# A searched order for attention and a gated MLP on one core: one early unit's q and k in another buffer, and all order keys drawn anew

## The chip, the cores and the metric

The kernel runs on one core of one Trainium2 chip. The metric is device time in microseconds (us), the median of three runs; the profile comes from one more execution, profiled on its own. The core has five engines: PE (TensorE, matmuls; its weight loads are shown apart as PEld), DVE (VectorE), ACT (ScalarE), POOL (GpSimd) and SP (SyncE, which here issues every DMA).

## The reference, cut to what matters

```python
# q, k, v: (8 batches, 8 heads, 576, 64), float32
scores = q @ k.T / 8                       # heads 0-3: band mask of width 32; heads 4-7: stride mask of 32
attn   = softmax(scores)                   # per row, with the maximum taken off
x      = attn @ v                          # (8, 576, 512) after joining the heads
h      = relu(x @ w_in)                    # w_in 512 x 1024
u, v_  = h[..., :512], h[..., 512:]
v_n    = (v_ - mean) / sqrt(var + 1e-6)    # over the 512 columns
v_s    = w_spatial @ v_n + b_spatial       # w_spatial 576 x 576
out    = (u * v_s) @ w_out                 # w_out 512 x 512
```

## The kernel before, in words

**Units.** Attention is cut into 32 units: unit t = 4 b + hp is head pair hp of batch b. hp 0 and 1 are local (band mask), hp 2 and 3 strided. A local unit's scores are the 72 small matmuls of L522 from its q and k, a strided one's the 64 of L666 from q and `kbd` (k spread over two halves of one tile, half t % 2). Softmax runs on ACT (ten L579 exponentials for a local unit, one L703 for a strided one) and on DVE (L474, L478, L483 normalise, L603 or L720 transposes into the single buffer `pc`). ACT and POOL then copy the transposed blocks to `ptl` or `pts` (L423 on ACT, L425 on POOL), PE multiplies with v into `po` (L632 local, L737 strided), and the result is split into two parts in `x` (an ACT cast L445, the remainder by DVE at L433).

**Batches.** A batch's four `x` are the left side of the v projection (L1034 on PE, 48 matmuls with the v half of `w_in`) and of the u projection (L1102, 96 matmuls with the u half). Then come normalisation, the spatial product (L1206 for batch 0, L1319 after it) and the output product (L1402). Products run on parts: an operand is rounded (L423 or L425) and its remainder kept (L433). The weights arrive in 8-byte words and are converted by L836 (ACT), L844 (POOL) and L852 (DVE), before the same two steps make their parts.

**The order.** Everything is put in a list of operations with their dependences. `Program.order` walks it with costs of its own; of the operations that are ready on an engine, the one with the lowest key goes first, and where an operation may run on several engines it takes the one that ends first. Keys and fetch times come from the table `KEYS` ("a" for units 0 to 7, "la" and "lb" when their loads are issued, "lv", "lu", "wv", "wu" for the weights, and offsets for later stages). The engines run this fixed order; each waits for its operands in turn. `fillers` puts matmuls of zeros (L1630) on PE ahead of an operation for which its plan has a gap.

**Buffers.** q, k and v of local units have one buffer each (rings `r_q`, `r_k`, `r_v`). The early units are declared in the order of their keys "a": 0, 2, 1, 3, 7, 4, 6, 5. Every second one of them among units 0 to 5 (2, 3, 4, 5) takes its q, k and v into slots of `vals`, the tile that appears as `w_out` in the rows, since the output weights come there later. The third early unit is unit 1; its q and k take the second turn of `r_q` and `r_k`, after unit 0. `v4` holds a batch's normalised v; batch 0's is written by L969 after the v projection.

Of the kernel before, what the change touches and what calls it, by code (L numbers as in the profile page):

```python
# [21 lines left out]
HF = DFF // 2  # L22
# [16 lines left out]
CST = 4 * STRIDE + RA + P  # L39
NT = 4  # L40
KEYS = {
    "a": (-48545.87, -36450.5, -36547.42, -23595.43, -3178.89, 14869.6, -2232.61, -3181.02,),
    "v": (10039.16, 14285.99, -10044.91, -16436.95,),
    "u": (11778.77, 13701.39, 14705.78, 15523.81,),
    "s": (-26158.74, 14643.81, 10992.75, 15205.58,),
    "t": (19117.6,),
    "o": (-36501.18, -36627.51,),
    "cst": (-27997.89,),
    "wv": (-36499.87, -14239.13, -2799.46, 1118.56,),
    "wu": (-16432.62, -14796.9, 11768.24, 15524.94,),  # L50
    "lead": (8.83,),
    "fill": (-7882.3, -28137.8, -18899.66, -36412.32, 14186.24, 14826.12,),
    "dp": (854.17, 114.16, 15736.62, 10572.35,),
    "dpt": (3807.98,),
    "lv": (-16503.38, -23194.14, -4424.27, 10590.77,),
    "lu": (18295.16, -11375.3, -4178.09, 15192.78,),
    "lo": (15846.06, -23588.61, 20391.52, 1117.83,),
    "ls": (29744.2, -10984.47, -15240.56, 11983.74, 21527.45,),
    "pre": (7.7, 138.52,),
    "hp": (0.05, 2.03, -16.53, -0.46,),  # L60
    "ol": (-4.44, -4.25, -2.31, -74.96, -289.07, -184.32, 8.51, -6.01,),
    "os": (7.25, 0.33, -27.58, 12.96, 14.34, 74.42, 8.53, 11.2,),
    "vo": (0.15,),
    "uo": (-12.97,),
    "so": (260.06, 79.44, 4.82,),
    "oo": (172.19, 63.89,),
    "to": (-58.13, -3.08, 424.65,),
    "near": (15258.77,),
    "ps": (10.91, -25.52,),
    "tp": (-81.08, 172.34,),  # L70
    "la": (-26458.74, -27118.44, -38717.9, -4867.1, 10591.01, 12736.6, 19276.04, -6157.7,),
    "lb": (-8992.74, -13792.93, -2075.65, -14235.35, 16095.89, 15151.06, -36506.16, -28599.87,),
}
WARM_END, WARM_GAP, WARM_COST, WARM_COLS, WARM_SHARE = 110000.0, 700.0, 427.0, 256, 0.8
PE_MASKED, APART = (0, 1, 2, 3), ()
# [286 lines left out]
def attention_moe(ctx, tc, qT, kT, ks, vl, vs, cst, w_in, w_out, wsp, wtail, out):  # L362
# [4 lines left out]
    ps = ctx.enter_context(tc.tile_pool(name="ps", bufs=1, space=PSUM))  # L367
# [3 lines left out]
    def f32(t):  # L371
        return t.bitcast(F32)
# [27 lines left out]
    r_v4 = Ring(sb, "v4", [P, NT, HF], F32, 1)  # L400
# [28 lines left out]
    def rest(key, n, dst, src, hi, reads, writes, engs=(DVE, POOL), extra=0):  # L429
        cost = {DVE: 70 + 1.04 * n + extra, POOL: 120 + 2.3 * n}  # L430

        def fn(eng):
            eng.tensor_tensor(dst(), src(), f32(hi()), op=ALU.subtract)  # L433

        add(
            key, [(e, cost[e]) for e in engs], fn, reads, writes,
            port=(DVE, POOL) if POOL in engs else (), kind=1,
        )
# [12 lines left out]
    def load(key, dst, src, writes, nbytes, reads=()):  # L451
        add(key, [(DMA, nbytes / DMA_RATE)], lambda eng: eng.dma_start(dst(), src), reads, writes)
# [2 lines left out]
    vals = r_wo.new()  # L455
    early_units = []
    ahead_units = NHP + 2

    def evac_x(due, whole, x_t, o_ps, w, c0, src, dst, extra=0):
        if whole:  # L460
            evac(due - 1, w, lambda: f32(dst(0)), src, [(o_ps,)], [(x_t, 0, c0)], extra=extra)
            return
        evac(due - 1, w, lambda: dst(0), src, [(o_ps,)], [(x_t, 0, c0)], extra=extra)
        rest(
            due - 0.5, w, lambda: dst(1), src, lambda: dst(0),
            [(o_ps,), (x_t, 0, c0)], [(x_t, 1, c0)], (DVE,), extra,
        )
# [291 lines left out]
    def attention(t, due):  # L759
        b, hp = divmod(t, NHP)  # L760
        local = hp < 2
        n = len(early_units)
        early_units.append(t)
        spare = n % 2 and t < ahead_units

        def home(ring, name, width):
            if not spare:
                buf = ring.new()
                return buf, [(buf,)]
            at = VALS + {"q": 0, "k": SP, "v": SP + STRIDE + S}[name]  # L770
            return Slot(vals, lambda w: f32(w).rearrange("p a b c d -> p (a b c d)")[:, at : at + width]), [
                (vals, name)
            ]

        q, qtok = home(r_q, "q", SP)
        if t == 2:
            place = r_t[0].new()
            vtok = [(place,)]
            v = Slot(place, lambda w: f32(w).rearrange("p a b c -> p (a b c)")[:, : NU * D].rearrange(
                "p (u d) -> p u d", d=D  # L780
            ))
        else:
            v, vtok = home(r_v, "v", NU * D)
            if spare:
                v = Slot(v, lambda w: w.rearrange("p (u d) -> p u d", d=D))
        fetch_k, fetch_v = (KEYS[n][t] if t < len(KEYS[n]) else due - d for n, d in (("la", 33), ("lb", 20)))
        load(fetch_k - 1, q, qT[b, hp], qtok, P * SP * 4)
        k = None
        if local:
            k, kin = home(r_k, "k", STRIDE + S)  # L790
            load(fetch_k, k, kT[b, hp], kin, P * (STRIDE + S) * 4)
            load(fetch_v, lambda: v()[:, : 2 * LB, :], vl[b, hp], vtok, P * 768 * 4)
        else:
            for j in range(2):
                load(
                    fetch_k, lambda j=j: kbd[j::2, t % 2, j, STRIDE:],
                    ks[b, hp - 2, j], [("k", t % 2, j)], 64 * S * 4, [("k0", t % 2)],
                )
            load(fetch_v, v, vs[b, hp - 2], vtok, P * 1024 * 4)
            kin = [("k", t % 2, j) for j in range(2)]  # L800
        (local_attention if local else strided_attention)(t, due, q, k, v, vtok, kin, qtok)

    def x_tok(t):
        return [(xs[t], i, c0) for i in range(1 if t in WHOLE else 2) for c0 in ((0, 3) if t % NHP < 2 else (0, 1))]
# [211 lines left out]
    def turn(b):  # L1016

        return sorted(range(NHP), key=lambda hp: due(NHP * b + hp))

    def v_tile(key, step, x_at, m, toks, kts, b=None):  # L1020
        v_ps = r_pm.new(held)
        for n, kt in enumerate(kts):
            val, vtok = in_value(1, kt)
            whole = b is not None and NHP * b + kt in WHOLE
            given = [vtok] if whole else [("w_in", 1, kt, 0), ("w_in", 1, kt, 1)]

            def f(eng, n=n, kt=kt, val=val, whole=whole):
                if whole:
                    eng.matmul(
                        v_ps()[:m, :], f32(x_at(kt)[:, 0, :]), val(), start=n == 0, stop=n == NT - 1,  # L1030
                    )
                    return
                for i, (a, w) in enumerate(PROD):
                    eng.matmul(  # L1034
                        v_ps()[:m, :],
                        x_at(kt)[:, a, :],
                        w_in_sb[:, w, kt, HF:],
                        start=(n == 0 and i == 0),
                        stop=(n == NT - 1 and i == 2),
                    )  # L1040

            add(
                key + step * n, [(PE, whole_cost(512) if whole else 3 * pe_cost(m, 512))], f,
                toks(kt) + given, [(v_ps,)],
                spare=None if n else (v_ps, v_ps),
            )
        return v_ps

    vns, v4s, tls, us = {}, {}, {}, {}

    def flat(u):
        return u() if u.ring is r_u else f32(u()).rearrange("p a b -> p (a b)")
# [1 line left out]
    def by_tile(buf):  # L1054
        return lambda w: buf()[:, w].rearrange("p a b -> p (a b)")[:, :HF]
# [2 lines left out]
        return lambda: v4()[:, 2 * j : 2 * j + 2, i * HF // 2 : (i + 1) * HF // 2]  # L1058

    def project_v(b, key):  # L1060
        v4 = v4s[b] = r_v4.new()
        if b not in FAST_S:
            vns[b] = [(r_g if i < NT - 1 else r_t[2]).new() for i in range(NT)]
        for i in range(NT):
            k0 = key + 2.6 * i
            v_ps = v_tile(
                k0, 0.65,
                lambda kt, i=i: xs[NHP * b + kt]()[:, :, i * P : i * P + P],
                P, lambda kt: x_tok(NHP * b + kt), turn(b), b,
            )  # L1070
            v = lambda i=i: v4()[:, i]
            chain(k0 - KEYS["vo"][0], v_ps, P, v, [(v4, i, 0), (v4, i, 1)], b > 0 and i in ACT_NORM)
            if b not in FAST_S:
                at, buf = by_tile(vns[b][i]), vns[b][i]
                rnd(k0, HF, lambda at=at: at(0), v, [(v4, i, 0), (v4, i, 1)], [(buf, 0)])
                rest(
                    k0, HF, lambda at=at: at(1), v, lambda at=at: at(0),
                    [(v4, i, 0), (v4, i, 1), (buf, 0)], [(buf, 1)],
                )
# [433 lines left out]
    lead = min(nb, 2)  # L1513
# [199 lines left out]
```

## Time and profile before

| | |
|---|---|
| median of three runs | 512.02 us (510.07 to 512.26) |
| the profiled execution, its own time | 512.99 us |
| its span, first to last instruction | 511.2 us |
| PE busy | 489.7 us, 96% of the span |
| DVE, ACT, POOL busy | 381.3, 302.9, 183.4 us |
| mean granted TensorE clock | 0.983 |

The profiled execution takes 1.8 us more than its span, and 0.97 us more than the median. [...]

### The profile page before, as it was taken

What the parts mean: (1) busy time and instruction counts of PE and PEld (TensorE: products, weight loads), DVE (VectorE), ACT (ScalarE), POOL (GpSimd) and SP (SyncE); (2) the same over time, 40 slices, a digit from 0 to 9 for tenths busy, and PEclk for the clock granted to TensorE, in tenths of its full rate; (3) what the DMA queues carried; (4) which work ended last, traced back from release to release, by engine and by line L of the source; (5) the groups of instructions that cost most, each with busy time, mean ns of one, the idle gap of its engine ahead of it and who ended that gap; (6) DMA issues with size and microseconds to landing.
All of it is one profiled execution on the core that took longest, in us unless ns stands there. A gap on an engine that the chain in (4) does not pass through costs nothing.

```text
span 511.2 us, 15881 instructions
## 1 busy us (share of the span) xinstructions
PE 489.7 (96%) x6316; PEld 447.3 (88%) x6316; DVE 381.3 (75%) x1119; ACT 302.9 (59%) x935; POOL 183.4 (36%) x298
## 2 busy tenths in 40 slices
PE   7489999999999999999999999999999999999996
PEld 4367989898897999989998999989998999889996
DVE  3868887699998866999288964999469852966175
ACT  4857685777567777547555676637654643334333
POOL 4753541323655741545125240445216121222010
PEclk9579999999999999999999999999999999999999
DMA  8957132642513542506040252504120040002002
GB/s 312 401 204 257 44 107 84 223 131 90 184 50 96 174 115 81 167 2 196 20 129 0 76 198 81 161 7 158 59 80 1 9 171 1 1 0 94 1 1 94
DMA packets 26970, 54.48 MB, mean 107 GB/s; under 512 B 3216, under 2 KB 11536, under 8 KB 26896
## 3 DMA queue, kind: packets, MB, share of 16 engines
q1 hardware_dynamic: 26896, 53.47, 32.2%
q8 instruction: 50, 0.82, 0.7%
q14 instruction: 24, 0.20, 0.1%
HBM read 44.02 MB, written 9.44 MB: 105 GB/s over the span
## 4 chain that ended last, share of the span: by engine, by line
PE 77%; DVE 9%; DMA 5%; POOL 2%; ACT 2%; issue 2%; SPq 1%; DVEq 0%; POOLq 0%; ACTq 0%
PE m L1102 18%; PE m L1034 16%; PE m L1402 15%; PE m L1319 13%; PE po L632 3%; PE po L737 3%; PE m L1206 2%; DMA q<-qT 2%; PE s L522 2%; PE m L1173 2%; PE s L666 2%; PE m L1174 2%; DMA g<-w_in 1%; DVE g L433 1%; DVE g L867 1%
## 5 line engine op out<-in xcount | busy, mean ns | idle before, releaser
L1102 PE MATMUL m<-x,w_in_sb 128*128 128x288 f32 x768 | 104.6, 296 | 0.6 <-issue 0.6
L1102 PEld LDWEIGHTS m<-x,w_in_sb 128*128 128x128 f32 x768 | 102.7, 189 | 1.4 <-issue 0.8
L1034 PE MATMUL m<-w_in_sb,x 128*128 128x512 f32 (+1 forms) x408 | 101.2, 404 | 0.0
L1402 PE MATMUL m<-g,w_out 128*128 128x288 f32 x672 | 95.1, 298 | 2.1 <-DVE o L1425 0.9
L1402 PEld LDWEIGHTS m<-g,w_out 128*128 128x128 f32 x672 | 90.5, 188 | 5.2 <-DVE g L433 1.5
L1034 PEld LDWEIGHTS m<-w_in_sb,x 128*128 128x128 f32 (+1 forms) x408 | 75.9, 189 | 19.2 <-DVE x L433 0.3
L423 ACT CAST g<-u 128x288 fp32r<-128x288 f32 x85 | 36.2, 433 | 34.7 <-DVE u L867 16.6
L1319 PE MATMUL m<-wsp_sb,g 128*128 128x288 f32 x336 | 51.2, 298 | 0.1
L579 ACT ACTIVATE pl<-pl,ml 128x64 f32<-128x64 f32 (+1 forms) x140 | 47.1, 340 | 2.8 <-DVE ml L559 2.6
L425 POOL TENSOR_SCALAR ptl<-pc 32x64 f32<-32x64 f32 (+3 forms) x95 | 37.2, 392 | 31.4 <-DVE pc L603 14.7
L1319 PEld LDWEIGHTS m<-wsp_sb,g 128*128 128x128 f32 x336 | 46.6, 188 | 1.2 <-ACT u L445 0.3
L433 DVE TENSOR_TENSOR x<-po,x 128x288 fp32r<-128x288 f32 x64 | 26.9, 445 | 24.5 <-ACT x L445 24.3
L987 POOL TENSOR_TENSOR bn<-bn,sel 128x1 f32<-128x1 f32 (+1 forms) x37 | 23.0, 625 | 61.7 <-DVE bn L982 57.7
L433 DVE TENSOR_TENSOR g<-u,g 128x288 fp32r<-128x288 f32 x77 | 38.4, 519 | 3.5 <-ACT g L423 1.8
L1319 PE MATMUL m<-wsp_t,g 128*128 128x288 f32 x252 | 39.6, 296 | 1.1 <-ACT o L445 1.1
L423 ACT COPY ptl<-pc 32x320 f32<-32x320 f32 (+3 forms) x97 | 34.4, 356 | 10.2 <-DVE pc L603 8.5
L1116 ACT ACTIVATE u<-m 128x288 f32<-128x288 f32 x56 | 22.3, 408 | 30.4 <-PE m L1102 29.5
L433 DVE TENSOR_TENSOR g<-v,g 128x512 fp32r<-128x512 f32 x40 | 27.6, 691 | 13.5 <-ACT g L423 9.6
L969 ACT ACTIVATE v<-m 128x512 f32<-128x512 f32 x32 | 18.8, 597 | 31.0 <-PE m L1034 30.5
L1319 PEld LDWEIGHTS m<-wsp_t,g 128*128 128x128 f32 x252 | 35.4, 188 | 1.5 <-ACT o L445 1.3
L445 ACT CAST x<-po 128x288 fp32r<-128x288 f32 x60 | 22.2, 398 | 22.9 <-PE po L632 11.9
L445 ACT COPY o<-m 128x288 f32<-128x288 f32 x74 | 29.1, 398 | 8.7 <-PE m L1319 7.0
(168 smaller groups left out, 856.3 us busy)
## 6 DMA issues: line engine op xcount, KB each, us to landing
q<-qT SPq DMA_DIRECT2D x28, 295.0 KB, 3.3
v_raw<-vs SPq DMA_DIRECT2D x14, 512.0 KB, 4.1
v_raw<-vl SPq DMA_DIRECT2D x14, 384.0 KB, 3.7
kbd<-ks SPq DMA_DIRECT2D x32, 144.0 KB, 3.8
outT<-o SPq DMA_DIRECT2D x32, 144.0 KB, 3.0
k<-kT SPq DMA_DIRECT2D x14, 304.0 KB, 4.6
outT<-u SPq DMA_DIRECT2D x28, 144.0 KB, 2.5
g<-w_in SPq DMA_DIRECT2D x5, 512.0 KB, 5.9
```

The costliest lines, as they stand in the source:

```text
L423: eng.copy(dst(), src())
L425: eng.tensor_scalar(dst(), src(), 1.0, 0.0, op0=ALU.mult, op1=ALU.add)
L433: eng.tensor_tensor(dst(), src(), f32(hi()), op=ALU.subtract)
L445: eng.copy(dst(), src())
L579: eng.activation(p_sb()[:m, u, :], src, AF.Exp, bias=st()[:m, u : u + 1], scale=SCALE if masked else -1.0, **total,)
L969: lambda eng: eng.activation(v()[:m], v_ps()[:m, :], AF.Relu), [(v_ps,)], toks,
L987: lambda eng: eng.tensor_tensor(bn()[:m, 9:10], bn()[:m, 8:9], sel[:m, 0:1], op=ALU.pow),
L1034: eng.matmul(v_ps()[:m, :], x_at(kt)[:, a, :], w_in_sb[:, w, kt, HF:], start=(n == 0 and i == 0), stop=(n == NT - 1 and i == 2),)
L1102: eng.matmul(u_ps()[:, :HS], w_in_sb[:, w, kt, f * P : (f + 1) * P], xs[NHP * b + kt]()[:, a, r], start=(n == 0 and i == 0), stop=(n == NT ...
L1116: lambda eng, u=u, f=f, u_ps=u_ps: eng.activation(flat(u)[:, f * HS : (f + 1) * HS], u_ps()[:, :HS], AF.Relu),
L1319: eng.matmul(banks[j]()[:, :HS], buf()[:, a, r, P * j : P * j + P], at(w, r), start=first and r == 0 and i == 0, stop=tail is None and r = ...
L1402: eng.matmul(o_ps()[:, :HS], w_out_t[0]()[:, w, r, BLOCKS[name], j * P : (j + 1) * P], at(a), start=(first and r == 0 and i == 0), stop=(r ...
```

## The change

Two things change. First, unit 1's q and k go to a buffer that is idle until the v projection of batch 0 writes it: `v4`. The ring turn of `r_q` and `r_k` that they leave falls to the next unit that asks for one. Second, all numbers of `KEYS` are others. Shapes, formulas and the list of operations stay as they are. Lines below the new code move down (L579 is L580, L1034 is L1039, L1102 is L1109, L1630 is L1637).

```diff
-    "a": (-48545.87, -36450.5, -36547.42, -23595.43, -3178.89, 14869.6, -2232.61, -3181.02,),
+    "a": (-44893.87, -34918.54, -34921.08, -31255.24, -3190.06, 13718.87, -503.41, -3191.92,),
...
-    "la": (-26458.74, -27118.44, -38717.9, -4867.1, 10591.01, 12736.6, 19276.04, -6157.7,),
+    "la": (-44251.4, -34909.86, -37998.29, -4144.15, 13982.3, -34242.77, -34705.02, -39685.72,),
...
+    v4s = {0: r_v4.new()}
...
         def home(ring, name, width):
+            if n == 2 and name != "v":
+                i = "qk".index(name)
+                flat_v = lambda w: w.rearrange("p a b -> p (a b)")[:, 2 * HF * i : 2 * HF * i + width]
+                return Slot(v4s[0], flat_v), [(v4s[0], 2 * i + r, j) for r in range(2) for j in range(2)]
...
-    vns, v4s, tls, us = {}, {}, {}, {}
+    vns, tls, us = {}, {}, {}
...
     def project_v(b, key):
-        v4 = v4s[b] = r_v4.new()
+        if b not in v4s:
+            v4s[b] = r_v4.new()
+        v4 = v4s[b]
```

**The loads on SP.** The first loads of the program, before, from the conversion of the first weight block on; `q_188` and `k_190` are unit 1's, `u`, `g` and `wsp_t` take weights, `x` takes rows of `wsp`, `w_out` is `vals`:

```order
L452 DMA u_102<-w_in 128x1024
L452 DMA kbd<-ks 64x576 x2
L452 DMA g_107<-w_in 128x1024
L452 DMA x_113<-wsp 128x576
L452 DMA w_out_84<-vs 128x1024
L452 DMA u_132<-w_in 128x1024
L452 DMA x_142<-wsp 128x576
L452 DMA v_raw_180<-vl 128x768
L452 DMA kbd<-ks 64x576 x2
L452 DMA q_188<-qT 128x590
L452 DMA k_190<-kT 128x608
```

The first loads of the changed program; unit 1's are those into `v_0_124`, the `v4` tile:

```order
L1548 DMA cst_sb<-cst 128x274
L452 DMA q_89<-qT 128x590
L452 DMA k_95<-kT 128x608
L452 DMA g_98<-w_in 128x1024
L452 DMA w_out_103<-qT 128x590
L452 DMA kbd<-ks 64x576 x2
L452 DMA x_111<-wsp 128x576
L452 DMA v_0_124<-qT 128x590
L452 DMA v_0_124<-kT 128x608
L452 DMA x_138<-wsp 128x576
```

Unit 1's k is the ninth load instead of the fifteenth (a row marked x2 is taken as one), and one weight block stands ahead of it instead of three.

**PE around the first product with v.** Before, the end of unit 1's scores, unit 0's product with v, the scores of unit 3, the first v projection matmuls and unit 2's product with v:

```order
L522 MATMUL m_137<-k_190,q_188 32x64
L632 MATMUL po_328<-ptl,v_raw_180 64x96 x6
L632 MATMUL po_339<-ptl,v_raw_180 64x96 x6
L666 MATMUL m_140<-kbd,w_out_84 32x36 x32
L1034 MATMUL m_400<-w_in_sb,x_352 128x512 x3
L737 MATMUL po_412<-pts,wsp_t_0_231 64x2x18
```

The same place of the changed program:

```order
L523 MATMUL m_135<-v_0_124 32x64
L1637 MATMUL po_334<-zeros 32x256 x10
L633 MATMUL po_334<-ptl,v_raw_198 64x96 x6
L633 MATMUL po_355<-ptl,v_raw_198 64x96 x6
L667 MATMUL m_140<-kbd,w_out_103 32x36 x32
L1039 MATMUL m_419<-w_in_sb,x_367 128x512 x3
L738 MATMUL po_426<-pts,wsp_t_0_180 64x2x18
```

Ten rows of zero matmuls now stand between unit 1's scores and unit 0's product. Those that stood further on (three rows and two, around the scores of units 7 and 4) are two rows now; in all there are 20 such rows instead of 13. The numbers of all other matmuls are equal line by line.

**ACT after unit 0's softmax.** Before, from the copies of unit 0's transposed blocks (`pc_274`) to the first two exponentials of unit 1 (`m_134`, `m_137`):

```order
L423 COPY ptl<-pc_274 32x10x32 x3
L423 COPY ptl<-pc_274 32x8x32
L423 COPY ptl<-pc_274 32x4x32
L423 COPY ptl<-pc_274 32x2x32
L423 CAST w_in_sb<-w_out_84 128x512
L836 ACTIVATE g_228<-g_228 128x512
L445 CAST x_352<-po_328 128x288
L445 CAST x_352<-po_339 128x288
L423 COPY pts<-pc_346 32x16x18 x3
L579 ACTIVATE pl_77,ml_79<-m_134,ml_79 128x64
L579 ACTIVATE pl_77,ml_79<-m_137,ml_79 128x64
```

The same place of the changed program (`m_132` and `m_135` are unit 1's scores):

```order
L423 COPY ptl<-pc_300 32x10x32 x3
L423 COPY ptl<-pc_300 32x8x32
L423 COPY ptl<-pc_300 32x4x32
L423 COPY ptl<-pc_300 32x2x32 x2
L580 ACTIVATE pl_77,ml_79<-m_132,ml_79 128x64
L423 CAST wsp_sb<-x_138 128x2x288
L580 ACTIVATE pl_77,ml_79<-m_135,ml_79 128x64
```

Unit 1's exponentials now follow the copies at once; two casts of `wsp_sb` and, after the fifth of them, the two casts of unit 0's `x` lie between the ten. Between the copies of unit 1's own blocks and the casts of its `x`, ACT has five weight operations now, where there was one. On PE, the scores of unit 5 (36 pairs) now stand ahead of the first L1102, where they stood after the 24th; from there on the order on PE is the same but for places at which attention units cut in. Over the whole program DVE has 30 operations more (15 of L433, 8 of L867, 4 of L483 among them), POOL 29 two-input ones fewer and 9 of L425 more, ACT 11 casts and copies fewer.

## Rows read from the trace of the kernel before

**Rows 1.** Windows: us, busy time (instructions) of PE, PEld, DVE, ACT, POOL; clock, DMA share, GB/s.

```profile
10.00:20.00 10.00, 1.49 (x89) 1.16 (x75) 8.71 (x19) 7.45 (x30) 6.03 (x8) 0.65 1.03 406
20.00:30.00 10.00, 7.76 (x159) 6.58 (x160) 6.75 (x15) 7.07 (x31) 7.52 (x12) 0.67 1.04 395
99.00:146.00 47.00, 45.34 (x569) 41.32 (x568) 44.87 (x124) 33.97 (x96) 20.57 (x24) 1.00 0.39 126
215.55:333.01 117.46, 116.88 (x1566) 109.10 (x1565) 89.71 (x274) 71.07 (x228) 41.80 (x69) 1.00 0.31 95
```

**Rows 2.** What PE waited for over the whole span: us in total, times, longest.

```profile
PE m L522 <- DMA k<-kT: 7.7, 1, 7.7
PE po L737 <- issue: 2.2, 1, 2.2
```

**Rows 3.** PE in order of time: start us, us, line, tiles, count, wait before.

```profile
17.89 1.34 PE L522 MATMUL m<-k,q 64*32 64x64 f32 x72 [7.74 <-DMA k<-kT]
20.00 2.19 PE L632 MATMUL po<-ptl,v_raw 128*64 128x96 f32 x24 [0.77 <-POOL ptl L425]
28.34 7.49 PE L1034 MATMUL m<-w_in_sb,x 128*128 128x512 f32 x21
37.92 1.21 PE L632 MATMUL po<-ptl,v_raw 128*64 128x96 f32 x24
49.69 3.35 PE L1102 MATMUL m<-x,w_in_sb 128*128 128x288 f32 x24
52.97 1.14 PE L737 MATMUL po<-pts,v_raw 64*64 64x36 f32 x64
54.04 0.97 PE L522 MATMUL s<-w_out 64*32 64x64 f32 x72
444.85 11.27 PE L1034 MATMUL m<-w_in_sb,x 128*128 128x512 f32 x48
```

**Rows 4.** ACT, POOL and DVE in order of time, 17 to 35 us.

```profile
17.47 0.65 ACT L423 CAST wsp_sb<-x 128x576 fp32r<-128x576 f32 x1
18.05 2.43 ACT L423 COPY ptl<-pc 32x320 f32<-32x320 f32 x6
21.61 0.37 ACT L445 CAST x<-po 128x288 fp32r<-128x288 f32 x1
23.88 0.32 ACT L579 ACTIVATE pl<-m,ml 128x64 f32<-128x64 f32 x1
24.18 0.30 ACT L579 ACTIVATE pl<-m,ml 128x64 f32<-128x64 f32 x1
30.00 0.21 ACT L579 ACTIVATION_READ_ACCUMULATOR pl<-m,ml 64x1 f32 x1
33.09 3.01 POOL L425 TENSOR_SCALAR ptl<-pc 32x320 f32<-32x320 f32 x6
17.16 0.80 DVE L603 STREAM_TRANSPOSE pc<-pl 128x640 f32<-128x640 f32 x1
```

**Rows 5.** Windows as in rows 1, after PE's two idle stretches.

```profile
13.00:14.00 1.00, 0.00 (x0) 0.00 (x0) 0.09 (x1) 1.00 (x7) 0.84 (x3) 0.50 1.03 394
28.00:30.00 2.00, 2.00 (x15) 1.64 (x12) 1.23 (x3) 1.66 (x10) 0.32 (x1) 0.50 1.05 396
```

**Rows 6.** DMA issues, 0 to 45 us: tiles, count, KB each, median us to landing.

```profile
v_raw<-vl SPq DMA_DIRECT2D x2, 384.0 KB, 6.3
w_out<-kT SPq DMA_DIRECT2D x2, 304.0 KB, 6.9
```

**Rows 7.** The issue of unit 1's v on SP.

```profile
25.36 0.33 SPq L452 DMA_DIRECT2D v_raw<-vl  x1
```

**Rows 8.** DVE and POOL in order of time, at 130 and 56 us.

```profile
130.49 1.52 DVE L483 TENSOR_TENSOR pp<-pp,mx 128x288 f32<-128x288 f32 x1
130.41 1.29 POOL L867 TENSOR_TENSOR v<-v 128x512 f32<-128x512 f32 x1
56.03 0.46 DVE L483 TENSOR_TENSOR pp<-pp,mx 128x288 f32<-128x288 f32 x1
```

More of the change, by code (lines that the diff above doesn't have):

```diff
@@ L41 @@
 KEYS = {
-    "a": (-48545.87, -36450.5, -36547.42, -23595.43, -3178.89, 14869.6, -2232.61, -3181.02,),
[L43 to L70, printed above, removed]
-    "la": (-26458.74, -27118.44, -38717.9, -4867.1, 10591.01, 12736.6, 19276.04, -6157.7,),
-    "lb": (-8992.74, -13792.93, -2075.65, -14235.35, 16095.89, 15151.06, -36506.16, -28599.87,),
+    "a": (-44893.87, -34918.54, -34921.08, -31255.24, -3190.06, 13718.87, -503.41, -3191.92,),
@@ new lines @@
+    "v": (-2810.29, -12128.07, -1687.49, -26558.84,),
+    "u": (15964.95, 29527.72, 31760.64, 13043.35,),
+    "s": (-48288.31, -44892.86, -43645.28, -36128.68,),
+    "t": (42175.42,),
+    "o": (-1614.63, -5723.49,),
+    "cst": (-45514.64,),
+    "wv": (-44071.37, -32108.45, 46701.81, 53190.54,),
+    "wu": (44641.61, 14489.25, -184.6, -43642.99,),
+    "lead": (7.63,),
+    "fill": (14244.08, 13201.8, -35181.89, -35007.95, -2621.23, -4291.2,),
+    "dp": (1227.9, 12.48, 13438.64, 63416.92,),
@@ new lines @@
+    "dpt": (5145.73,),
+    "lv": (-41706.16, 19747.99, -26450.31, 44752.58,),
+    "lu": (44814.44, 13716.43, -34900.79, 45439.75,),
+    "lo": (44767.72, -36135.43, -26015.77, 14700.03,),
+    "ls": (-1873.27, -35726.72, -3193.89, -29206.82, 38692.31,),
+    "pre": (0.98, 201.19,),
+    "hp": (1.46, 17.46, -19.6, -1.05,),
+    "ol": (-4.81, -1.97, -83.56, -15.28, -397.63, -173.59, 15.76, -6.31,),
+    "os": (9.38, 7.77, -42.16, 23.46, 13.5, 112.89, -7.83, -202.64,),
+    "vo": (-10.95,),
+    "uo": (122.84,),
@@ L73 @@
+    "so": (146.17, 90.75, 224.33,),
+    "oo": (32.37, 5.7,),
+    "to": (-84.46, -4.52, 320.0,),
+    "near": (57359.77,),
+    "ps": (2.8, -110.71,),
+    "tp": (-462.02, 508.05,),
+    "la": (-44251.4, -34909.86, -37998.29, -4144.15, 13982.3, -34242.77, -34705.02, -39685.72,),
+    "lb": (-2534.85, 13906.78, -7006.51, 42261.49, -45191.78, -40284.21, 13014.5, -747.88,),
 }
```

## The prediction

> **What bounds the kernel now.** I read the windows first, then PE's waits, then the order in time on each engine. PE is busy 489.7 of 511.2 us. In the steady batches it has nothing left to give: in the 117.46 us of two batches it works 116.88 [rows 1]. Nearly all that can be won lies in the first 50 us: from 10 to 20 us PE works 1.49 us, and its one long wait of the program is 7.74 us for the k of unit 1 [rows 1 to 3]. After that it is slow as well as late: the granted clock is 0.65 to 0.67 between 10 and 30 us [rows 1], and 21 matmuls of the v projection take 7.49 us, 357 ns each, where 48 at full clock take 11.27, 235 ns each [rows 3]. A wait of 2.2 us with no releaser lies in unit 2's product with v [rows 2]. The DMA engines are full from 10 to 30 us, at 395 to 406 GB/s [rows 1], so what comes first in SP's order comes first on the chip. A second tight place is 99 to 146 us, where DVE works 44.87 of 47 us and PE loses 1.66 [rows 1].
>
> **Unit 1's q and k.** What stands ahead of and with unit 1's k in SP's order is, by the sizes of the loads, 5214 KB before (q and k of unit 0, q and v of unit 2, two kbd pairs, three weight blocks, two of wsp, unit 0's v, the constants) and 2718 KB after. The 2496 KB between them are 2.56 MB; at 406 GB/s that is 6.3 us. k landed when PE's wait ended, at 17.89 [rows 3], and so should land at 11.6. Unit 2's scores end at about 10.1 (17.89 less the wait), so PE waits some 1.5 us, not 7.74, and unit 1's scores end near 12.5. This alone moves nothing that PE must finish later: unit 0's product, next in order, waits for its softmax.
>
> **Unit 0's product.** Its transpose starts at 17.16 [rows 4], behind other steps of DVE. One weight step of about 0.7 us has gone from ahead of it and a reduction of unit 1 of half that has come. I take 0.4 us sooner, so PE starts it at 19.6, not 20.00.
>
> **Unit 1's softmax is the real term.** Before, its first exponential runs at 23.88, after the copies, two weight steps, two casts of x and three copies for unit 2; its last accumulator read ends at 30.21 [rows 4]. Now ACT copies seven blocks at 405 ns each (2.43 us for six [rows 4]) from 17.6 on, to 20.4. Then come ten exponentials at 0.30 (23.88 to 24.18 is one step), two wsp casts at 0.65 and two x casts at 0.37: 3.0 + 1.3 + 0.75 [rows 4], which ends at 25.45, 4.8 us sooner. From there to the end of the copies of unit 1's blocks it took 5.9 us before (30.21 to 33.09 + 3.01 [rows 4]); the same now gives 31.3. Unit 1's v has the same bytes ahead of it as before, about 10.5 MB, and was issued at 25.36; with 6.3 us to landing it comes at 31.7 [rows 6, 7]. I take 31.5 for unit 1's product, against 37.92 [rows 3], where PE came 1.8 us after the copies because it was held up by the slow v projection.
>
> **From there to the u projection.** PE's work, at full clock: the products of units 1 and 3 at 1.1 each, scores of units 4 and 5 at 0.9 (unit 5's row has 0.97, with the overlap into what follows [rows 3]), those of units 7 and 6 at 0.8 (64 matmuls for 72), and 24 matmuls at 235 ns, 5.6: 11.2 in all. One wait is new: the casts of unit 1's x stand behind five weight steps on ACT of about 0.6 us. They can't start before 34.3 (31.3 + 3.0), while PE is through with unit 7's scores at 33.4; with the casts and the remainder, PE waits 1.5. So the first L1102 starts at 31.5 + 11.2 + 1.5 = 44.2. Before it is 49.69, and unit 5's scores, 0.9, are still to come at 54.04 [rows 3]. The gain at this landmark is 5.5 + 0.9 = 6.4 us. Its bounds: PE's own work from 19.6, with nothing waited for, is 11.2 + 8.6 (two products 2.2, unit 3's scores 0.8, 24 matmuls 5.6) and 0.9 of zeros, which ends at 40.3, a gain of 10.3; and if the 2.2 us and the low clock (below) come back in full, it is 1.5.
>
> **The clock.** The zeros after unit 1's scores are 20 instructions, 4.3 us at full clock, so they end at 16.8 and PE then idles until 19.6. [...] Unit 0's product took 2.19 at the low clock where unit 1's took 1.21 [rows 3]; over some 5.5 us of low clock that is 2.75 us of work lost. Most of it lies under the wait for unit 1's softmax and for ACT's five steps, which ends at 34.3 whatever PE does; I charge 0.6, between 0 and 2.75. [...]
>
> **Unit 5's scores.** They stand ahead of the whole u projection now, and PE works in order: 96 matmuls wait behind them, and DVE's and ACT's work on u behind those. Their q and k go to slots that unit 4's scores free, 5.6 us of matmuls and 0.7 of unit 6's scores earlier. Issued one after the other, the second lands 6.9 us after [rows 6] at the pace of the full queue, and in about 4 when it isn't full. I charge 0.5, between 0 and 2.
>
> **DVE from 99 to 146 us.** Everything in it hangs on weights whose buffers PE frees, so it moves with PE. It holds about three operations more, 0.45 each, 1.35 us; against that, by the order, five of POOL's steps fewer run beside it. A normalising step took 1.52 us beside a POOL step, 0.46 elsewhere [rows 8]. [...] I charge 0, from -1.66 (PE's loss there gone) to +1.35.
>
> **The rest.** From 150 us on PE does the same matmuls; the 27 or so DVE operations that come in addition, some 13 us, fall on an engine that is busy 89.71 of 117.46 us [rows 1], under PE's work. I charge 0.
>
> **The sum.** -6.4 + 0.6 + 0.5 = -5.3 us: 512.99 becomes 507.7 for an execution like the profiled one, and 512.02, the median, 506.7.
>
> **The rivals.**
> - *The front gives less*, because the 2.2 us come back as they were (the wait stands where small matmuls follow each other while the DMA engines are full, which is still so) and the clock costs its whole 2.75. Then 6.4 - 2.2 - 2.75 + 1 for what is hidden under ACT = 2.45, less 0.5: about 510.
> - *The front gives more*: softmax of unit 1 isn't held by v or by ACT, PE runs through from 19.6. With 8 to 10 us, about 503. Against it speaks that v's bytes come no sooner.
> - *The change doesn't do what it seems to*: the gain of the front is lost again between 60 and 150 us, because DVE has no slack there (rows 1 give 2.13 us in 47). Then 512. Against it: the work there starts when PE frees buffers, and DVE idles much before 50 us.
> - *Slower*: the work taken from POOL makes DVE the bound of the steady batches. It decides if DVE's 89.71 us per two batches, with 3 to 4 more, come to stand in front of PE: each operation on which PE then waits adds its 0.45 us. Half of the 27 would cost 6 us and undo the front; all of them, 12, gives 518.5. PE's idle time there, 0.58 in 117.46, shows no sign of it.
>
> **How the numbers follow.** What a measurement of this kernel can tell from no change is about 0.5%, 2.56 us. The forecast (505 to 508.5) has 0.55; less from the front (508.5 to 511) 0.20, of which half is under 509.46; more from the front 0.10; the gain lost later 0.08; slower 0.07. Faster is then 0.55 + 0.10 + 0.10 = 0.75, same 0.18, slower 0.07. The range leaves the last two cases out and a part of the second: 501.5 to 510.8. The likeliest case alone is 505 to 508.5.
>
> **What would show it.** PE's wait for k gone or under 2 us; unit 1's product at 30 to 33 us; the first L1102 at 42.5 to 46; the clock at 0.50 for a few us after 19; the span from the first L1102 to the end equal to before less 0.9 us, within 1.5. I am wrong if unit 1's product comes after 35, if PE waits over 2 us for unit 5's q or k, or if PE's idle time after 60 us grows by more than 2 us.

## The result, and the profile after

| | median, us | runs |
|---|---|---|
| kernel before, measured beside it | 509.95 (509.24 to 512.26) | 6 |
| changed kernel | 514.75 (514.43 to 516.46) | 6 |

The ratio is 1.0088, with a 95% interval of 1.0061 to 1.0115: slower by 4.8 us, where 506.7 was forecast. The profiled execution took 514.52 us, with a span of 512.7.

The front went much as forecast. PE's order in time, changed kernel, from the end of the first scores to the u projection (start, length, engine, line, operation, tiles, count, and the wait before it):

```profile
10.93 0.80 PE L523 MATMUL m<-v 64*32 64x64 f32 x59 [1.07 <-DMA v<-kT]
15.25 0.46 PE L523 MATMUL m<-v 64*32 64x64 f32 x13 [3.52 <-issue]
15.64 6.25 PE L1637 MATMUL po<-zeros 128*32 128x256 f32 x20
21.83 1.21 PE L633 MATMUL po<-ptl,v_raw 128*64 128x96 f32 x24
...
26.57 5.18 PE L1039 MATMUL m<-w_in_sb,x 128*128 128x512 f32 x21
...
32.66 1.21 PE L633 MATMUL po<-ptl,v_raw 128*64 128x96 f32 x24
...
44.91 0.97 PE L523 MATMUL s<-w_out 64*32 64x64 f32 x72
45.81 2.65 PE L1109 MATMUL m<-x,w_in_sb 128*128 128x288 f32 x18
```

The tile that holds unit 1's q and k goes by the name `v` here. Against [rows 3], the wait for k is 1.07 us, not 7.74; unit 1's product starts at 32.66, not 37.92; the u projection at 45.81, not 49.69, with unit 5's scores done. One line should have puzzled me: 20 zero matmuls took 6.25 us and ended at 21.8, where I had them end at 16.8.

The loss is later. PE's waits over the whole program, changed kernel (what PE waited for, total us, times, longest):

```profile
PE po L738 <- DMA v_raw<-vs: 3.6, 3, 2.0
PE m L523 <- issue: 3.5, 1, 3.5
PE m L1409 <- DVE g L433: 1.6, 3, 0.7
...
PE po L738 <- DVE ml L560: 0.9, 1, 0.9
PE s L523 <- issue: 0.9, 1, 0.9
PE po L633 <- DMA v_raw<-vl: 0.7, 1, 0.7
```

The first line has no counterpart in [rows 2], nor among the other waits of the kernel before: three times PE waits, in a strided unit's product, for the load of its v. Two more waits of this kind stand in other lines. One is the last line, of a local unit, at 169.81 us. The other is the 0.9 us put down to `DVE ml`, at 300.07 us: that product reads no `ml`, and its v landed at 299.94. It starts 0.14 us after that landing, as the other four start 0.13 to 0.14 us after theirs. The five waits add up to 5.2 us. The longest, in PE's order around 237 us, and behind it SP's order there:

```profile
229.60 1.21 PE L633 MATMUL po<-ptl,v_raw 128*64 128x96 f32 x24
230.74 1.85 PE L1409 MATMUL m<-g,w_out 128*128 128x288 f32 x12
232.43 2.93 PE L1109 MATMUL m<-x,w_in_sb 128*128 128x288 f32 x21
237.35 1.70 PE L738 MATMUL po<-pts,v_raw 64*64 64x36 f32 x64 [1.98 <-DMA v_raw<-vs]
238.98 1.15 PE L523 MATMUL s<-k,q 64*32 64x64 f32 x61
241.02 0.45 PE L523 MATMUL s<-k,q 64*32 64x64 f32 x11 [0.90 <-issue]
241.41 5.62 PE L1109 MATMUL m<-x,w_in_sb 128*128 128x288 f32 x30
246.96 1.14 PE L738 MATMUL po<-pts,v_raw 64*64 64x36 f32 x64
```
```profile
229.70 0.34 SPq L452 DMA_DIRECT2D q<-qT  x1
230.14 0.85 SPq L1440 DMA_DIRECT2D outT<-o  x2
231.10 0.42 SPq L452 DMA_DIRECT2D v_raw<-vs  x1
231.61 0.91 SPq L1440 DMA_DIRECT2D outT<-o  x2
232.65 0.84 SPq L1440 DMA_DIRECT2D outT<-u  x2
233.55 1.66 SPq L452 DMA_DIRECT2D kbd<-ks  x2
```

`v_raw` is one buffer. It comes free when the product before it ends, at 230.8 (229.60 + 1.21); the load is issued at 231.10, and PE has only 4.6 us of other matmuls until 235.4. The load lands at 237.21, 6.1 us after its issue, among a q load, six stores of 144 KB and two key loads. In the kernel before, unit 17's product stands ahead of the v projection, and the same load has 15.7 us until unit 18's product (PE, then SP):

```profile
209.87 1.21 PE L632 MATMUL po<-ptl,v_raw 128*64 128x96 f32 x24
215.39 11.27 PE L1034 MATMUL m<-w_in_sb,x 128*128 128x512 f32 x48
228.20 1.14 PE L737 MATMUL po<-pts,v_raw 64*64 64x36 f32 x64
```
```profile
212.45 0.52 SPq L452 DMA_DIRECT2D v_raw<-vs  x1
```

The new keys put unit 17's product behind the projection (208.1 to 219.3 us in the changed kernel), and so next to unit 18's. A short hand-over alone is not yet a wait: at 289.56 the kernel before ends such a product and starts the next at 293.96 without one. Its load, the first transfer issued on SP since 265 us, took 3.9 us.

In the changed kernel the low clock follows the wait: the strided product at 237.35 takes 1.70 us, not the 1.14 of the one at 246.96. The windows say why (us, length, PE busy and instructions, granted clock, of which 1.00 is full speed, DMA share, GB/s):

```profile
236.00:238.00 2.00, 0.65 (x35) 0.92 0.99 361
238.00:240.00 2.00, 2.00 (x101) 0.50 0.13 46
240.00:242.00 2.00, 1.10 (x22) 0.50 0.72 250
242.00:244.00 2.00, 2.00 (x11) 0.50 0.71 189
245.00:247.00 2.00, 2.00 (x20) 1.00 0.02 9
```

The clock falls to 0.50 some 0.3 us after the end of the wait (0.84 from 237 to 238 us) and stays there until 244.5 (0.75 from 244 to 245). To see what such places cost in all, I added up the matmuls that each traced execution had started by a given time, each at its spacing at full clock (a 288-column one 139 ns, a 512-column one 235, the small ones 12 to 50; zeros left out), and took off the same sum for the kernel before. This is the lead in us, here for the profiled executions of this change and of five experiments below:

```
at us   changed   e5 (before   e9 (no   e7 (place  e6 (products  e11 (new front,
        kernel     again)      zeros)    alone)       later)       old rest,
                                                                   2 moves)
  50      4.3        1.2        -0.4      -0.1         5.5           3.7
 150      5.9        2.0         0.0       0.0         7.1           5.1
 230      5.9        1.8        -0.4       0.0         7.5           4.9
 250     -0.2        2.1        -0.3       0.0         6.4           5.1
 310     -1.0        1.4        -0.5      -0.3         4.8           4.8
 370     -2.5        1.5        -1.0      -0.3         4.3           4.9
 500     -2.4        1.5        -1.1      -0.3         3.0           4.4
```

The changed kernel leads by 5.9 us until 230, loses 6.1 of it by 250, 0.8 more by 310 (0.91 us at 300.07 and 0.19 at 305.60, both for loads of v) and 1.5 by 370 (1.46 for a load of v at 360.22; there the clock stays at 1.00). A trace is one execution: the front of the changed kernel, of e6 and of e11 is the same, and yet the three lead by 5.9, 7.1 and 5.1 us at 150.

### The profile page after: what moved, and what is told of

Same layout as the page of the kernel before. It is cut to its first block, busy times and chain, and to the rows that moved or that the text cites. A ratio compares the mean times of both kernels' runs of the same rounds, so it can differ in the third digit from the quotient of the medians.

```text
span 512.7 us, 15896 instructions
## 1 busy us (share of the span) xinstructions
PE 492.5 (96%) x6330; PEld 448.2 (87%) x6330; DVE 386.5 (75%) x1149; ACT 302.7 (59%) x926; POOL 155.9 (30%) x277
## 4 chain that ended last, share of the span: by engine, by line
PE 73%; DVE 12%; DMA 7%; issue 2%; ACT 2%; POOL 1%; SPq 1%; POOLq 0%; DVEq 0%; ACTq 0%
PE m L1039 16%; PE m L1109 16%; PE m L1326 14%; PE m L1409 11%; PE po L738 3%; DMA v_raw<-vs 3%; DVE g L433 3%; PE po L633 2%; PE s L523 2%; PE m L1213 2%; DMA g<-w_out 2%; PE m L1180 2%; PE m L1181 1%; PE po L1637 1%; DVE g L872 1%
## 5 line engine op out<-in xcount | busy, mean ns | idle before, releaser
L1109 PE MATMUL m<-x,w_in_sb 128*128 128x288 f32 x768 | 107.9, 299 | 0.0
L1109 PEld LDWEIGHTS m<-x,w_in_sb 128*128 128x128 f32 x768 | 104.1, 191 | 1.2 <-issue 0.2
L1039 PE MATMUL m<-w_in_sb,x 128*128 128x512 f32 (+1 forms) x408 | 98.6, 397 | 0.4 <-DVE x L433 0.4
L1409 PE MATMUL m<-g,w_out 128*128 128x288 f32 x672 | 94.0, 297 | 2.7 <-DVE g L433 1.6
L1039 PEld LDWEIGHTS m<-w_in_sb,x 128*128 128x128 f32 (+1 forms) x408 | 74.4, 185 | 19.3 <-DVE x L433 0.8
L425 POOL TENSOR_SCALAR ptl<-pc 32x64 f32<-32x64 f32 (+3 forms) x100 | 38.9, 389 | 62.0 <-DVE pc L604 29.8
L580 ACT ACTIVATE pl<-pl,ml 128x64 f32<-128x64 f32 (+1 forms) x140 | 47.1, 339 | 3.2 <-DVE ml L560 2.9
L433 DVE TENSOR_TENSOR g<-v,g 128x512 fp32r<-128x512 f32 x44 | 30.9, 704 | 16.0 <-ACT g L423 13.1
L433 DVE TENSOR_TENSOR g<-u,g 128x288 fp32r<-128x288 f32 x85 | 38.2, 466 | 2.7 <-POOL g L425 1.4
L992 POOL TENSOR_TENSOR bn<-bn,sel 128x1 f32<-128x1 f32 (+1 forms) x37 | 24.1, 655 | 51.6 <-DVE bn L987 39.7
L445 ACT CAST x<-po 128x288 fp32r<-128x288 f32 x58 | 21.8, 400 | 28.0 <-PE po L633 14.0
L433 DVE TENSOR_TENSOR x<-po,x 128x288 fp32r<-128x288 f32 x64 | 27.3, 446 | 12.1 <-ACT x L445 12.0
L423 ACT COPY ptl<-pc 32x320 f32<-32x320 f32 (+3 forms) x92 | 33.1, 360 | 4.1 <-DVE pc L604 2.3
L423 ACT CAST g<-v 128x512 fp32r<-128x512 f32 x34 | 21.1, 621 | 21.1 <-PE m L1326 8.5
```

The lines of the kernel that those rows point to most:

```text
L423: eng.copy(dst(), src())
L425: eng.tensor_scalar(dst(), src(), 1.0, 0.0, op0=ALU.mult, op1=ALU.add)
L445: eng.copy(dst(), src())
L580: eng.activation(p_sb()[:m, u, :], src, AF.Exp, bias=st()[:m, u : u + 1], scale=SCALE if masked else -1.0, **total,)
L992: lambda eng: eng.tensor_tensor(bn()[:m, 9:10], bn()[:m, 8:9], sel[:m, 0:1], op=ALU.pow),
L1039: eng.matmul(v_ps()[:m, :], x_at(kt)[:, a, :], w_in_sb[:, w, kt, HF:], start=(n == 0 and i == 0), stop=(n == NT - 1 and i == 2),)
```

## The experiments

Except for e5, the order is written out as a table, operation by operation, taken from the planner of one kernel or the other, and edited there; the planner no longer chooses:

```diff
-        issued = self.order()
-        fillers = self.fillers(issued)
+        issued, fillers = written(), FILLS
```

With the table in it, line numbers in their rows are 81 higher (L738 is L819, L1109 is L1190). No run leaves work out. With the moved operations of PE, a few of ACT or DVE move too (e6, e8, e11, e13), and two or three output stores on SP (e8, e11, e13). Medians, each with the kernel before on the same chip (509.7 to 510.0 us in each set):

| run | us | runs | ratio to before, 95% |
|---|---|---|---|
| e1 new front, old rest | 509.88 | 12 | 0.9992 (0.9968 to 1.0016) |
| e2 old front, new rest | 522.0 | 4 | 1.0209 (1.0163 to 1.0256) |
| e3 new, stores later | 511.7 | 10 | 1.0035 (1.0005 to 1.0064) |
| e4 new, 16 zeros in the wait | 514.29 | 10 | 1.0074 (1.0047 to 1.0102) |
| e5 before again | 512.05 | 1 | |
| e6 new, products later | 511.25 | 10 | 1.0022 (1.0001 to 1.0042) |
| e7 old, placement alone | 511.75 (511.23 without one at 516.0) | 10 | 1.0024 (0.9997 to 1.0051) |
| e8 as e1, scores later | 507.58 | 12 | 0.9952 (0.9933 to 0.9971) |
| e9 as e8, no zeros | 511.89 | 12 | 1.0036 (1.0014 to 1.0059) |
| e10 new, 8 zeros in the wait | 512.58 | 10 | 1.0047 (1.0021 to 1.0072) |
| e11 as e8, a product later too | 506.1 | 6 | 0.9923 (0.9892 to 0.9953) |
| e12 e7 with 20 zeros | 511.21 | 12 | 1.0022 (0.9994 to 1.0051) |
| e13 e12 with e11's two moves | 507.73 | 12 | 0.9968 (0.9948 to 0.9987) |
| e14 as e11, 14 zeros | 510.04 | 12 | 0.9984 (0.9958 to 1.0011) |

**Front or rest? e1, e2.** The two orders are joined at about 150 us of the planner's time; what one had not yet done by then follows in the other's order.

> The new kernel's order up to about 150 us, then the order of the kernel before for all that is left. Theory A (the front gains 5 us and keeps them; the new order loses them at three places after 230 us, where PE waits for a v load): 504 to 506 us beside 509.95 for the kernel before. Rival B (whatever the front wins is taken back in the steady batches, because another engine or the queue sets their pace): 509 to 511.

> The other way round: the kernel before up to about 150 us, then the new order. Theory A (the loss belongs to the later order and doesn't depend on the lead; it is 5.9 us between 230 and 250 us and about 2.4 more by 370): 516.5 to 518.5 us. Rival B (the steady batches only absorb a lead that the front made): 510 to 512, no worse than before.

e2's profiled execution, 517.69, is where theory A put it: by the sum of the table above, its lead goes from 4.8 us at 230 to -4.4 at 500. Its three others, and so its median, are above A's range, at 521.4 to 524.2. Their mean granted clock is 0.977 to 0.980 against 0.987, which means 7 to 11 us more at 0.50, by an estimate from unit 0's product (2.19 us at 0.50, 1.21 at 1.00) some 3 to 5 us of work; where that happens no trace shows. So the new rest costs time whatever stands before it. But e1 is no faster than the kernel before: A fails there. In its traced execution (511.5 us, 1.6 above the median) the lead stays at 5.2 to 5.5 us from 150 to 270 and is 0.6 by 310. PE's order there, and the DMA queues during the wait (packets, MB, share):

```profile
290.20 0.90 PE L604 MATMUL s<-k,q 64*32 64x64 f32 x69 [0.35 <-DMA q<-qT]
293.13 0.42 PE L604 MATMUL s<-k,q 64*32 64x64 f32 x3 [2.04 <-issue]
```
```profile
q1 hardware_dynamic: 544, 0.85, 97.2%
q8 instruction: 1, 0.02, 2.6%
```

In the middle of unit 24's scores PE waits 2.04 us for nothing that a semaphore shows, while the data queue holds 97.2% of the DMA engines and one 16 KB packet of instructions comes through; the clock is 0.88 from 291 to 293 us, and 0.50 from 293 to 298 (for 6.8 us in all). I call such waits instruction waits, after that packet (the expectations of e9 and e13: waits for instructions); that PE waits for it is not shown. The lead is lost at one place, not worn down.

**The load: e3, e6.**

```diff
 SP order, at both places (units 18 and 26)
-  q, store o x2, v_raw, store o x2, store u x2, kbd x2, v_raw, q, k
+  q, v_raw, kbd x2, store u x2, v_raw, q, k, store o x4
```

> The new kernel, with the output stores that surround two v loads of strided units (issued at 231.10 and 354.49) put behind later loads in SP's order. Theory A1 (the load lands late, after 6.1 us, because it shares the DMA engines with six stores): it lands in 4 to 4.5 us, PE's waits of 1.98 and 1.46 us and the 0.50 clock after the first are gone, 506.5 to 508.5 us. Rival B1 (the order asks for the product too soon after the buffer comes free, the stores don't matter): the waits stay over 1 us and the time is 513.5 to 515.

Neither, quite: at 354 us the wait shrinks from 1.46 to 0.18 us, at 237 only from 1.98 to 1.23. There the load still takes 5.6 us, not 6.1, with the q load just ahead and the key loads just behind: the stores are a small part of its time. What the larger part is was not tested. The clock stays at 1.00 (the product takes 1.14 us and the 30 u matmuls behind the scores 4.24, not 1.70 and 5.62), and 3.0 us come back.

```diff
 PE order, at both places
-  product 18, scores 20, u x7 groups, ...
+  u x7 groups, product 18, scores 20, ...
-  product 19, scores 21, u x8 groups
+  u x8 groups, product 19, scores 21
```

> The new kernel with nothing changed in SP's order, but with the two strided products and the scores behind them put 7 to 9 groups of u matmuls later in PE's order, in the two batches where PE waited 1.98 and 1.46 us. Theory A (PE comes to the product sooner than a load issued 5 us earlier can land; nothing else is wrong): both waits and the 0.50 clock at 237.7 go, 507.5 to 510 us. Rival B (the later work is short of something else, and the loss comes back at another place): 513 to 515.

The two waits are gone and the clock doesn't fall (unit 18's product, at 236.52, takes 1.14 us; the mean clock is 0.993 against 0.987); 3.5 us come back. The median, 511.25, is 1.25 us above A's range, so A is right about the waits and wrong that nothing else costs. Its trace still shows, beyond 200 us, waits of 0.20 (243), 0.23 (245) and 0.58 us (294) for loads, of 0.49 for DVE (267 and 386) and 0.36 for ACT (369), and behind 430 us the three that the kernel before has too. The one at 294 goes by `DVE ml` again; its v landed at 294.34 and the product starts at 294.48.

**The clock after the wait: e4, e10.** Zeros (L1637) go ahead of unit 18's product, as the planner does in the front. "8" in e4's text became 16 instructions, 3.64 us, too long by 1.7; e10 has 8.

> The new kernel with 8 zero matmuls in PE's order ahead of the strided product that waits 1.98 us, so that PE works through most of that wait. Theory A2 (of the 6.1 us lost there 3 to 4 are the clock of 0.50 that follows, the wait itself is the smaller part): the clock stays 1.00 and the time is 510.5 to 512. Rival B2 (the wait and what it delays are the whole loss): 514 to 515.5.

> The new kernel with zeros ahead of the product that waits 1.98 us, half as many as in the run with zeros before: 8 instructions, some 1.8 us, as long as the wait itself. If the clock that fell after the wait is worth 2.6 to 3.5 us: the clock is 1.00 from 237 to 245 us and the time 511 to 512.5 us. If the earlier zeros only moved the loss: 514 to 515.

PE in e10, same place:

```profile
236.48 1.91 PE L1718 MATMUL po<-zeros 128*32 128x256 f32 x8
238.33 1.14 PE L819 MATMUL po<-pts,v_raw 64*64 64x36 f32 x64
239.40 0.76 PE L604 MATMUL s<-k,q 64*32 64x64 f32 x53
240.95 0.41 PE L604 MATMUL s<-k,q 64*32 64x64 f32 x19 [0.79 <-issue]
241.29 4.24 PE L1190 MATMUL m<-x,w_in_sb 128*128 128x288 f32 x30
245.47 1.14 PE L819 MATMUL po<-pts,v_raw 64*64 64x36 f32 x64
```

From the product to the next one it is 7.14 us, where the changed kernel takes 9.61 (246.96 - 237.35), with nearly the same instruction wait: the low clock alone cost 2.4 us (2.47 less 0.11 of instruction wait), more than the wait of 1.98. The median fell by 2.2, a little short of the first theory's range. e4 keeps the clock at 1.00 there as theory A2 says (1.14 us for the product and 4.24 for the 30 u matmuls, as in e10), but its median, 514.29, falls into B2's range: the same gain less the overrun of 1.7 would be 0.5, and that is what it gives, too little to tell from none with these runs.

**What the front is worth: e5, e7.**

> The kernel before, profiled a second time. Theory C (the profiled execution that the prediction was built on was a slow one: its clock fell a second time, at 26.6 us, and that is 3 to 4 us of the front that most executions don't lose): the clock stays 1.00 from about 22 us on, the first L1102 starts at 45 to 47 us and the span is 506 to 508 us. Rival D (that front is the kernel's own): the first L1102 at 49 to 50 us and a span near 511.

> The order of the kernel before, with q and k of the third early unit in the v buffer and their two loads put where the change has them, ahead of the weights in SP's order; nothing else moves. By the prediction's step (the wait for k alone holds up nothing that PE must finish later, since the product of unit 0 waits for its softmax): PE's wait of 7.7 us for k is under 2 us, the product of unit 0 still starts at 19.5 to 20.5 us and the time is 509 to 510.5. Rival E (the wait for k holds the front): the first L1102 is 3 to 6 us earlier than in the kernel before and the time 504 to 507.

e7 is as the prediction's step had it: wait for k 1.51 us, unit 0's product at 20.11, the first L1102 at 49.80, no gain. Its median, 511.75, is above the step's range of 509 to 510.5, and its clock falls twice, as in the first trace (2.19 us for unit 0's product, 7.21 for the 21 matmuls behind unit 2's; the mean is 0.983 in both). e5 lies between, its span of 510.3 us nearer to D: the product with v of unit 2 waits 1.77 us without a releaser, the clock falls again at 27.2 (0.57 from 27 to 31 us), but for 3.4 us, not 6.8, and the first L1102 starts at 48.43. e2 begins with the same old order, and there the clock didn't fall a second time (0.92 from 20 to 30 us, 1.00 from 30 to 40; 5.42 us for the 21 matmuls), after a wait of 1.99 us in the same product:

```profile
26.20 0.89 PE L818 MATMUL po<-pts,wsp_t 64*64 64x36 f32 x43 [1.99 <-issue]
27.02 5.42 PE L1115 MATMUL m<-w_in_sb,x 128*128 128x512 f32 x21
...
34.55 1.21 PE L713 MATMUL po<-ptl,v_raw 128*64 128x96 f32 x24
...
45.87 3.35 PE L1183 MATMUL m<-x,w_in_sb 128*128 128x288 f32 x24
```

So one order gives 45.87, 48.43 and 49.69 for the same landmark. The execution that I predicted from was at the slow end: of 121 executions of the kernel before in the five sets, 6 took as long as its 512.99 us, and 11 had a mean granted clock as low as its 0.983 (511.05 to 514.21 us); the 74 at 0.988 and above have a median of 509.1.

**Out of the stall: e8, e11.**

```diff
 PE order of e1
-  scores 24, o x2 groups, u x6 groups
+  o x2 groups, u x6 groups, scores 24          (e8: 8 groups)
-  product 30, o x2 groups, u x3 groups
+  o x2 groups, u x3 groups, product 30         (e11: 5 groups, and e8's move)
```

> The mix of new front and old rest, with the scores of one unit (PE waited 0.35 us for its q at 290 us, then 2.04 us in the middle of them, and the clock fell) put 6 groups of matmuls later in PE's order. Theory F (such small matmuls stall when they meet a full DMA queue, and moved out of it they don't): no clock of 0.50 after 20 us, 507.5 to 508.7 us. Rival G (the mix has no more to give): 509.5 to 510.5, as without the move.

> The mix with the scores put later, and with one more move: the strided product that waited 1.02 us for its v at 405 us goes 5 groups of matmuls later. If such a wait costs its own length when the clock holds: 506.3 to 507 us, against 507.6; if it is covered by something else: 507.3 to 508.

Both came out as the first theory had it: no stall in those scores (all 72 in 0.97 us), no clock of 0.50 after the front (the mean clocks are 0.997 and 0.992, against e1's 0.987), and e11's 506.1, just under its range, beats both kernels. What cost e1 its lead was thus that one place; that the full DMA queue is what stalls it is not shown by this.

**The zeros: e9, e12, e13, e14.**

> The mix with the scores put later (507.6 us), without the 20 zero matmuls ahead of the product of unit 0. Theory H (the zeros are worth something: they keep PE working, so that the clock is 1.00 when the product begins, and the instructions of the next small matmuls are fetched meanwhile): without them the product of unit 0 starts at 19.5 to 20.5 us instead of 21.8, but at 0.50, PE waits 1.5 to 3 us for instructions in unit 2's product, the first L1102 comes 1.5 to 4 us later, 509 to 511.5 us. [...]

Theory H holds in what the trace shows of it, the low clock and the wait in unit 2's product; that instructions are fetched while the zeros run is not shown. The time is 0.4 us above its range. PE in e9:

```profile
15.74 0.46 PE L604 MATMUL m<-v 64*32 64x64 f32 x13 [3.64 <-issue]
19.54 2.19 PE L714 MATMUL po<-ptl,v_raw 128*64 128x96 f32 x24 [3.34 <-ACT ptl L504]
...
28.10 1.50 PE L819 MATMUL po<-pts,wsp_t 64*64 64x36 f32 x43 [1.95 <-issue]
29.53 7.19 PE L1120 MATMUL m<-w_in_sb,x 128*128 128x512 f32 x21
...
37.63 1.21 PE L714 MATMUL po<-ptl,v_raw 128*64 128x96 f32 x24
...
50.92 2.65 PE L1190 MATMUL m<-x,w_in_sb 128*128 128x288 f32 x18
```

Unit 0's product starts 2.3 us sooner than in the changed kernel, and yet all that follows is 5 us later: 0.50 again at 27.2, 7.19 us for the 21 matmuls that took 5.18. The first L1102 was expected 1.5 to 4 us later and is 5.1 later than in the changed kernel. The 20 zeros are worth 4.3 us (511.89 - 507.58).

> The order of the kernel before with two edits: q and k of the third early unit in the v buffer with their loads ahead of the weights (511.75 us alone), and the 20 zero matmuls ahead of the product of unit 0. Theory H (the placement opens a gap ahead of that product and the zeros in it are the front's whole gain): the clock is 1.00 from about 20 us on, the first L1102 starts at 45.5 to 47.5 us, 506.5 to 508.5 us. Rival J (the zeros need the other moves of the new order, of copies and loads, to pay): the first L1102 after 48 us and 509.5 to 512.

> The order of the kernel before with the placement, the 20 zero matmuls, and the two moves of the mix (scores behind 6 groups, product behind 5). Theory K (placement and zeros are most of the front's gain; alone they lost it again at 294 us, where PE waited 2.89 us for instructions in the same scores and the clock fell, and at 413 us): no clock of 0.50 after 20 us, 507 to 508.5 us, 1 to 2 above the mix with both moves (506.1). Rival L (the rest of the old order gives a lead back at whatever place comes next): 509.5 to 511.5.

In e12 the front does what H says (clock 1.00 from 20.1 on, first L1102 at 46.66), and the time what J says: a wait of 2.89 us without a releaser in unit 24's scores at 294 us and a clock of 0.50 from 293.1 to 300 (1.81 us for six matmuls that e13 does in 1.06) take it back, as in e1. With the two moves, e13 keeps it: 507.73. Placement, zeros and moves are thus 2.0 of the 3.6 to 3.9 us that e11 gains on the kernel before. The two moves alone, on the kernel before, were not run.

> The mix with both moves (506.1 us), with 14 zero matmuls in place of 20 ahead of unit 0's product, so that they end at about 20 us, when that product's operands are there, instead of 22. If the overrun of 2 us is paid in full and the clock still rises: 504.3 to 505.3. If what follows waits for other things anyway: 505.5 to 506.5. If the clock then stays at 0.50 as without zeros: 509 to 511.

The time is the third case's, but not by its reason: the clock rises at 18.95, the 14 zeros take 4.67 us and unit 0's product starts at 20.56, with 1.21 us. PE then waits 0.66, 0.54 and 1.05 us, and the clock falls at 25.8 in the profiled execution (6.99 us for the 21 matmuls that took 5.18). Two of the twelve executions, at 505.4 and 505.8, have the highest mean clocks of the set (0.996 and 0.992, the others 0.986 to 0.990); it is likely, but not traced, that theirs didn't fall.

## Why the prediction was wrong

- **"The rest ... I charge 0"** is the step that failed, by most. In the traced execution the lead goes from 5.9 us at 150 to -2.4 at 500: the new rest costs 8.3 us. The five waits for v make 5.2 of it, the low clock after the longest 2.4, and the wait at 241.02, which has no releaser, 0.9. By medians, e11, with the same front and the old rest with two moves, is 8.65 us faster (506.1 against 514.75). Against the old rest as it was the difference is 4.9 (e1), since that rest loses the lead too, at its one stall; so with it the forecast of 506.7 would also have failed. I looked at PE's share and at DVE's load, and not at the one-buffer `v_raw`, which each strided product needs reloaded a few us after the product before. That wait was in no rival. My own test says it too: in the windows from 60 to 500 us PE's idle time grew from 4.7 to 9.9 us, where more than 2 was to mean that I am wrong. Taking the two longest waits for v out gives back 3.5 us (e6), and holding the clock through the longest 2.2 (e10).
- **What e6 leaves.** After 150 us, e6's trace still loses 4.1 us of lead and e11's 0.7; the short waits explain 2.4 of these 3.4 (2.8 in e6, of which 1.5 for loads, against 0.45 in e11), and the rest is not settled. The medians lie further apart, by 5.1, than the traced executions: e6's took 508.74 us, 2.5 below its median, and e11's 507.44, 1.3 above.
- **"512.99 becomes 507.7 ... 512.02, the median, 506.7".** The base was one execution whose clock had fallen twice in the front. The kernel before has its median at 509.7 to 510.0 in all later sets, and its other traces of that order reach the first L1102 at 48.43 and 45.87. Measured against the median, the new front is worth 3.6 to 3.9 us (e11, its two moves included), not 5.3. That the front in the traces gains about what the sum says (4.3 us at 50, 5.9 at 150) is in part luck, since it is measured against that same execution.
- **"so they end at 16.8 and PE then idles until 19.6".** The zeros lasted until the product, which I had sized away: a wait of 3.52 us without a releaser put their start at 15.64, and with the clock at 0.50 until 19.2 the 20 of them take 6.25 us, not 4.3. They run to 21.8, so unit 0's product starts at 21.83 and not at 19.6; the clock is 1.00 from 19.2 on, where I expected 0.50. No run shows the 0.6 that I charged for the clock: it was my estimate from the clock of the kernel before [rows 3, 5]. What the runs showed in its place is that without the zeros, the low clock and the wait of 1.95 us in unit 2's product together cost 4.3 (e9). The clock of 0.50 came again after the wait of 1.98 us here and in the wait of 2.04 in e1; e10 prices one such fall at 2.4 us.
- **"Unit 1's softmax is the real term"** gave nearly the right time for a wrong reason, by luck. The copies ended at 31.2 (31.3 forecast) and the product started at 32.66 (31.5). But v, forecast at 31.7, landed at 32.21, and four zeros stand ahead of the product until 32.66. In e8, with the same front, the copies ended at 29.3 and v landed at 31.49; the zeros ended at 31.60 and the product started at 31.62. In e9 the copies ended at 32.3, and the product came at 37.63, with PE busy all the time from 28.10. The load of v or PE's own pace set that time, not the softmax.
- **Unit 1's q and k; unit 5's scores; DVE from 99 to 146.** These held. k's wait was 1.07 (1.5 forecast), and taking it away alone is worth nothing (e7); no wait for unit 5's operands; the lead went from 4.9 at 100 us to 5.9 at 150.
- **The rival that ended slower** named DVE. The sign was its, the mechanism wasn't: the waits that came in addition after 150 us were for loads of v, but for the 0.9 us at 241. DVE's two waits of 0.49 us have a part in what e6 leaves; moving those operations back to POOL was not tried.

## What to carry to other kernels

A lead won early reaches the end only if every later place with a tight hand-over keeps it; list the single buffers whose reload stands between two uses on the bound engine, and compare the time between the uses with the landing time of that load among the transfers around it. Price a wait of PE with the low clock that may follow it: here that was 2.4 us, more than the wait of 1.98, and zeros that cover a wait were worth 2.2 us (e10) and 4.3 (e9). Check a wait's label against the tiles that the instruction reads and against the landing times. Before a single profile serves as the base of a sum, see how far the program's own executions differ in the very stretch that the change touches.

## What was not expected of the hardware

- In the scores of units 1 and 20 the waits without a releaser stood at a place in the order of instructions and not at a time. In unit 1's it is ahead of the last 13 of 72 matmuls in the changed kernel, e7, e9 and e12 (3.52, 3.36, 3.64 and 2.82 us), and at the same place in the other traces with q and k in the v buffer (from 1.52 us in e8 to 4.29 in e10). In unit 20's it is ahead of the last 11 in the changed kernel and in e3; with 8 more instructions ahead, in e10, ahead of the last 19. In the changed kernel one 16 KB instruction packet fell in the first wait (12.75 us) and one 1.5 us ahead of the second (238.62). Between 10 and 20 us the DMA engines were full, at 400 GB/s; from 238 to 240 us, just ahead of the wait at 240.13, their share was 0.13, and over the wait itself 0.43.
- A wait of 1.4 to 1.7 us for a load was followed by 0.50 in two executions (1.57 us, e4 at 359 us; 1.67 us with 0.79 more close behind, e2 at 300 us, where the next 30 u matmuls take 5.56) and not in others (1.46 in the changed kernel, with 1.00 from 360 to 362 us; 1.63 in e10 and 1.62 in e3, at mean clocks of 0.993; 1.62 in e12). What decides it these traces don't show.
